# Computing a layernorm, linear-attention and feed-forward block with pairs of 64-row matmuls on TensorE

## The chip, the cores and the metric

The kernel runs on one core of one Trainium2 chip. The metric is the device time of one execution in microseconds (us). Lower is better. Repeated executions of one kernel on one chip mostly agree within 1 to 2%. Each call of experiments ran on its own chip, with the kernel before run between the others on the same chip. I therefore compare kernels of different calls by their ratio to the kernel before.

Engine names in the profile: PE is TensorE's matmul stream, PEld its weight loads, DVE VectorE, ACT ScalarE, POOL GpSimd. SP (SyncE) issues most DMAs.

## The reference, cut to what matters

```python
x  = A_x                                    # [1, 2048, 448] bf16
xn = layernorm(x)
# A: attention with a softmax feature map, 16 heads of 28
q, k, v = split(xn @ wqkv)                  # each 2048 x 448
pq, pk  = q @ w_phi[h], k @ w_phi[h]        # per head, 28 x 28
phi(p)  = concat(softmax(p), softmax(-p))   # 56 features a head
kv, z   = sum_s phi(pk) v,  sum_s phi(pk)
A = (phi(pq) @ kv / (phi(pq) @ z + 1e-6)) @ wo
# B: feed-forward
B = silu(xn @ w1) @ w2                      # 448 -> 1792 -> 448
out = x + A + B
```

The kernels fold `w_phi` into the q and k columns of `wqkv`, so pq and pk are direct products of xn. Six products over features remain: q, k, v, `wo` (all 448 to 448), ffn1 (448 to 1792) and ffn2 (1792 to 448).

## The kernel before

It records all operations, schedules them with a static list scheduler and emits each engine's stream. A matmul here uses up to 128 rows of TensorE's array (ffn2, `128*128` in the page). The 448 features are cut into 4 slices of 112 rows, so every product over 448 is four matmuls into one bank of PSUM, the memory that TensorE writes its results to. Some words used below: kv is the sum over tokens of phi(pk) times v, and of phi(pk) itself (z); KVZ is the step that readies both sums; U is phi(pq) times them; the fold is the product of `wqkv` and `w_phi`. A chunk is 512 tokens, and its exp phase is the work on q, k, v and kv, with ffn2 tiles in between. The late stage is U, `wo` and the last ffn2 tiles. Warm-up means matmuls whose results nobody uses. The parts that the argument touches:

```python
KT, KP = 4, 112
# ffn1: 4 matmuls of 256 or 512 tokens, one bank, one silu each
for kt in range(KT):
    e.matmul(hps, w1_sb[:, kt, ft*128:(ft+1)*128], xnT_sb[:, kt, tok0:tok0+ntok],
             start=(kt == 0), stop=(kt == KT - 1))
...
# k and v of a 128-token tile: 4 + 4 matmuls of 448 columns
e.matmul(pkb, xnT_sb[:, kt, t*128:(t+1)*128], Wfull[:, kt, D:2*D], ...)
e.matmul(vb,  xnT_sb[:, kt, t*128:(t+1)*128], Wfull[:, kt, 2*D:3*D], ...)
...
# q of 512 tokens, transposed by construction (weights stationary): 4 x 4 matmuls of 512
e.matmul(pqb, Wfull[:, kt, g*KP:(g+1)*KP], xnT_sb[:, kt, c*512:(c+1)*512], ...)
...
# kv and U: groups of four heads, 8 matmuls of 116 or 120 columns a tile (cross-head blocks masked)
# ffn2 of a tile: 14 matmuls of 128 rows x 448 columns; ACT evicts, POOL adds x
# wo of a tile: 4 matmuls of 448 columns into its own bank; DVE adds the ffn2 result
```

The softmax here doesn't subtract the row's maximum and nothing guards it: scores larger than these inputs give would overflow.

## Time and profile before

The median is 187.96 us (187.78 to 188.22, 5 runs). The profiled span is 185.7 us.

| | before |
|---|---|
| PE busy | 176.4 us, 95% of the span |
| ACT, DVE, POOL busy | 99.9, 96.0, 75.6 us |
| PE's share of the chain that ended last | 77% |
| a matmul of 448, 512 and 116 columns | 189, 215 and 53 ns |

From the page of the kernel before: the busy time of each engine, then the chain that ended last.

```profile
PE 176.4 (95%) x1272; PEld 105.1 (57%) x1272; DVE 96.0 (52%) x215; ACT 99.9 (54%) x197; POOL 75.6 (41%) x94
...
PE 77%; DVE 7%; DMA 6%; SPq 4%; POOL 2%; issue 1%; ACT 1%; POOLq 0%; DVEq 0%; ACTq 0%
```

A busy PE need not be at its full pace (below, pairs of 208 ns and of 109 ns both count as busy), so its pace has to be read from the timeline. Columns: start, length from the first start to the last modelled end, engine and line, operation, output and inputs, shapes, count.

```profile
70.65 0.92 PE L582 MATMUL psum<-Wfull,xnT_sb 112*128 112x448 bf16 x4
71.41 1.03 PE L627 MATMUL psum<-xnT_sb,Wfull 112*112 112x512 bf16 x4
72.27 0.92 PE L582 MATMUL psum<-Wfull,xnT_sb 112*128 112x448 bf16 x4
73.03 1.11 PE L640 MATMUL psum<-w_sb,hT 128*128 128x448 bf16 x5
73.98 0.92 PE L582 MATMUL psum<-Wfull,xnT_sb 112*128 112x448 bf16 x4
...
100.29 0.58 PE L604 MATMUL psum<-vaug,Ek 128*112 128x116 bf16 x8
100.71 0.54 PE L577 MATMUL psum<-Wfull,xnT_sb 112*128 112x448 bf16 x2
```

Take the distance between two starts and not the lengths, since the lengths overlap. Four matmuls of 448 columns take 71.41 - 70.65 = 0.76 us (chain view: the same), 189 ns each; four of 512 take 0.86 us, 215 ns each; eight of 116 take 0.42 us, 53 ns each. ffn2's five matmuls of 128 rows take 73.98 - 73.03 = 0.95 us, 190 ns each, like those of 112 rows. That is about 2.4 columns a nanosecond (2.2 for the short ones), and the number of rows in use does not enter. So the kernel pays for four slices of 112 rows what four slices of 128 would cost.

### The profile page before, as it was taken

To read this page: it belongs to the slowest core of one execution; us is meant where nothing else is said; L and a number is where in the kernel's file an instruction comes from. 1 tells how busy PE (TensorE), PEld (TensorE's weight loads), DVE (VectorE), ACT (ScalarE), POOL (GpSimd) and SP (SyncE) were. 2 spreads that over 40 slices of the span, in tenths; PEclk is the share of its full clock that TensorE was granted. 3 is DMA by queue.
4 is the path that set the end of the run, shared out by engine and by line. 5 is a ranking of instruction groups with operands and counts; after the bars stand their busy time and mean duration, and the time that the engine had idled before them with its cause. 6 is when DMAs were issued, how large, how long until landed. Compare 5 with 4: busy or idle time off the path is not lost.

```text
span 185.7 us, 3256 instructions
## 1 busy us (share of the span) xinstructions
PE 176.4 (95%) x1272; PEld 105.1 (57%) x1272; DVE 96.0 (52%) x215; ACT 99.9 (54%) x197; POOL 75.6 (41%) x94
## 2 busy tenths in 40 slices
PE   6978999999998999999999999999999999999982
PEld 6766866654444445556666666555555555555540
DVE  2439893050003000166777742478987888646762
ACT  2575496736663675838767765535444553513221
POOL 4136175000000000289888983165255235443651
PEclk9999999999999999999999999999999999999997
DMA  4999990000000000000000000001001000000011
GB/s 136 235 281 220 252 306 17 2 4 0 0 0 0 0 4 0 0 0 4 2 0 0 4 0 0 0 4 48 28 25 47 32 25 28 25 25 25 6 47 49
DMA packets 11375, 8.72 MB, mean 47 GB/s; under 512 B 992, under 2 KB 11360, under 8 KB 11360
## 3 DMA queue, kind: packets, MB, share of 16 engines
q1 hardware_dynamic: 11360, 8.51, 18.3%
q8 instruction: 10, 0.16, 0.4%
q14 instruction: 5, 0.04, 0.1%
HBM read 6.68 MB, written 1.84 MB: 46 GB/s over the span
## 4 chain that ended last, share of the span: by engine, by line
PE 77%; DVE 7%; DMA 6%; SPq 4%; POOL 2%; issue 1%; ACT 1%; POOLq 0%; DVEq 0%; ACTq 0%
PE psum L552 22%; PE psum L640 20%; PE psum L577 7%; PE psum L582 7%; DMA scr<-in_A_wqkv_dram 6%; PE psum L627 5%; PE psum L696 5%; SPq L445 4%; PE psum L604 4%; PE psum L660 3%; POOL scr L682 2%; DVE scr L676 2%; PE psum L688 2%; DVE den L669 1%; PE psum L513 1%
## 5 line engine op out<-in xcount | busy, mean ns | idle before, releaser
L552 PE MATMUL psum<-xnT_sb,w_sb 112*128 112x512 bf16 (+1 forms) x280 | 51.9, 337 | 0.8 <-ACT hT L555 0.5
L640 PE MATMUL psum<-w_sb,hT 128*128 128x448 bf16 x224 | 50.2, 352 | 0.8 <-DVE xnT_sb L541 0.6
L555 ACT ACTIVATE hT<-psum 128x256 bf16<-128x256 f32 (+1 forms) x70 | 34.4, 511 | 21.5 <-PE psum L552 21.0
L552 PEld LDWEIGHTS psum<-xnT_sb,w_sb 112*128 112x128 bf16 x280 | 26.4, 98 | 21.8 <-ACT hT L555 1.1
L645 POOL TENSOR_TENSOR Y_sb<-Y_sb,x_sb 128x448 f32<-128x448 f32 x16 | 16.5, 1033 | 52.9 <-ACT Y_sb L643 49.8
L592 DVE TENSOR_REDUCE Sk<-Ek 128x32 f32<-128x896 bf16 x16 | 17.3, 1084 | 28.4 <-ACT Ek L586 28.4
L682 POOL TENSOR_TENSOR scr<-scr 128x448 bf16<-128x448 f32 x16 | 18.1, 1134 | 33.7 <-DVE scr L676 25.3
L640 PEld LDWEIGHTS psum<-w_sb,hT 128*128 128x128 bf16 x224 | 21.0, 97 | 18.6 <-DVE xnT_sb L541 0.8
L596 POOL TENSOR_TENSOR Ek<-Ek,Rk 128x896 bf16<-128x896 bf16 x16 | 27.1, 1699 | 2.9 <-DVE Rk L594 1.7
L631 ACT ACTIVATE EqT<-psum 112x512 bf16<-112x512 f32 x32 | 17.6, 597 | 10.3 <-PE psum L627 10.3
L586 ACT ACTIVATE Ek<-psum 128x448 bf16<-128x448 f32 x32 | 15.6, 544 | 9.1 <-PE psum L577 5.0
L690 ACT ACTIVATE scr<-psum 112x512 bf16<-112x512 bf16 x16 | 9.5, 596 | 18.7 <-PE psum L688 18.7
L627 PE MATMUL psum<-xnT_sb,Wfull 112*112 112x512 bf16 x64 | 19.4, 379 | 0.0
L676 DVE TENSOR_TENSOR scr<-psum,Gq 128x896 f32<-128x896 f32 x16 | 17.4, 1090 | 0.7
L541 DVE COPY xnT_sb<-psum 112x512 bf16<-112x512 bf16 x12 | 4.8, 417 | 24.3 <-PE psum L535 24.3
L577 PE MATMUL psum<-Wfull,xnT_sb 112*128 112x448 bf16 x64 | 16.5, 352 | 0.0
L696 PE MATMUL psum<-wo_sb,scr 112*128 112x448 bf16 x64 | 14.8, 352 | 1.6 <-ACT scr L690 1.6
L643 ACT ACTIVATE Y_sb<-psum 128x448 f32<-128x448 f32 x16 | 8.8, 550 | 12.4 <-PE psum L640 5.8
L582 PE MATMUL psum<-Wfull,xnT_sb 112*128 112x448 bf16 x64 | 14.9, 352 | 0.0
L699 DVE TENSOR_TENSOR scr<-psum,Y_sb 128x448 bf16<-128x448 f32 x16 | 9.9, 620 | 6.9 <-POOL Y_sb L645 2.3
L521 DVE BATCH_NORM_STATS2 st<-x_sb 128x6 f32<-128x448 bf16 x16 | 9.6, 605 | 6.9 <-DMA x_sb<-in_A_x_dram 6.9
L665 DVE RECIPROCAL R<-psum 128x32 f32<-128x32 f32 x16 | 5.7, 357 | 11.7 <-PE psum L660 11.7
(48 smaller groups left out, 179.1 us busy)
## 6 DMA issues: line engine op xcount, KB each, us to landing
out_dram<-scr SPq DMA_DIRECT2D x16, 112.0 KB, 1.7
w_sb<-in_B_w_dram SPq DMA_DIRECT2D x7, 224.0 KB, 5.7
w_sb<-in_B_w_dram SPq DMA_DIRECT2D x1, 1568.0 KB, 14.9
x_sb<-in_A_x_dram SPq DMA_DIRECT2D x3, 448.0 KB, 8.1
scr<-in_A_wqkv_dram SPq DMA_DIRECT2D x1, 784.0 KB, 10.3
Wfull<-in_A_wqkv_dram SPq DMA_DIRECT2D x1, 392.0 KB, 10.3
wo_sb<-in_A_wo_dram SPq DMA_DIRECT2D x1, 392.0 KB, 11.0
x_sb<-in_A_x_dram SPq DMA_DIRECT2D x2, 112.0 KB, 2.4
```

The lines of the kernel that those rows point to most:

```text
L552: P.op("pe", d_mm(ntok), lambda e, lhsT=lhsT, rhs=rhs, hps=hps, kt=kt: e.matmul(hps, lhsT, rhs, start=(kt == 0), stop=(kt == KT - 1)), rea ...
L555: P.op("act", d_act(ntok), lambda e, dsth=dsth, hps=hps: e.activation(dsth, hps, ACTF.Silu), reads=[hps], writes=[dsth], table="silu", nam ...
L577: P.op("pe", d_mm(D), lambda e, lhsT=lhsT, rhs=rhs, pkb=pkb, kt=kt: e.matmul(pkb, lhsT, rhs, start=(kt == 0), stop=(kt == KT - 1)), reads= ...
L582: P.op("pe", d_mm(D), lambda e, lhsT=lhsT, rhs=rhs, vb=vb, kt=kt: e.matmul(vb, lhsT, rhs, start=(kt == 0), stop=(kt == KT - 1)), reads=[lh ...
L592: P.op("dve", d_dve(896), lambda e, E3=E3, sl=sl: e.tensor_reduce(Sk[:, sl, :], E3, AXL.X, ALU.add), reads=[E3], writes=[Sk[:, sl, :]], na ...
L596: P.op("pool", d_pool(896, 1.77), lambda e, E3=E3, sl=sl: e.tensor_tensor(E3, E3, Rk[:, sl, :, None].broadcast_to([128, 32, DH]), ALU.mult ...
L627: P.op("pe", d_mm(512), lambda e, lhsT=lhsT, rhs=rhs, pqb=pqb, kt=kt: e.matmul(pqb, lhsT, rhs, start=(kt == 0), stop=(kt == KT - 1)), read ...
L631: P.op("act", d_act(512), lambda e, dstE=dstE, pqb=pqb, s=s: e.activation(dstE, pqb, ACTF.Exp, scale=(1.0 if s == 0 else -1.0)), reads=[pq ...
L640: P.op("pe", d_mm(D), lambda e, lhsT=lhsT, rhs=rhs, ft=ft: e.matmul(fb, lhsT, rhs, start=(ft == 0), stop=(ft == FT - 1)), reads=[lhsT, rhs ...
L676: P.op("dve", d_dve(896), lambda e: e.tensor_tensor(dsto, U4[:, :, :, 0:DH], Gq[:, q, :].rearrange("p (s h) -> p s h", s=2)[:, :, :, None] ...
L682: P.op("pool", d_pool(448, 2.26), lambda e: e.tensor_tensor(o_sum[:, q, :], o_both[:, q, 0, :], o_both[:, q, 1, :], ALU.add), reads=[o_bot ...
L696: P.op("pe", d_mm(D), lambda e, lhsT=lhsT, rhs=rhs, g=g: e.matmul(ob, lhsT, rhs, start=(g == 0), stop=(g == G - 1)), reads=[lhsT, rhs], wr ...
```

## The change

The intent is to fill the array. The 448 features are cut into seven slices of 64 rows. The operands lie in both halves of the partitions, and two matmuls that use rows 0 to 63 and rows 64 to 127 and write two different banks are issued as a pair. If both run at once, one product over 448 costs 3.5 passes instead of 4. What else moves:

- q and k are one pair with tokens stationary. q then has to be transposed, which DMA does (16 times), as it does for xT of 12 of the 16 token tiles.
- Heads are handled in pairs of 56 features, so kv and U have 58 and 29 columns.
- POOL normalises q as well as k; this replaces the row sums that U carried before.
- ffn2's half sums of the late tiles stay in PSUM, and wo adds onto one of them.
- The scheduler keeps PE's order as written and places the other engines by latest start times.

The diff, cut to its core:

```diff
-        KT, KP = 4, 112
+    NS = D // 64
+        def pair(mms, n, name, dur=None):
+            def fn(e):
+                for (dst, lhsT, rhs, st, sp) in mms:
+                    ins = e.matmul(dst, lhsT, rhs, start=st, stop=sp, skip_group_check=True)
+                return ins
 ...
-            for kt in range(KT):                      # ffn1
-                lhsT = w1_sb[:, kt, ft * 128:(ft + 1) * 128]
+            for s in range(NS):
+                pair([(bank(2 * sl + q)[:, 0:n], w1_sb[HALF[q], s, i * 128:(i + 1) * 128],
+                       xT[HALF[q], c % NXC, s, j0 * 128:j0 * 128 + n], s == 0, s == NS - 1) for q in range(2)], n, "f1")
+            act(dst, src, ACTF.Silu, 2 * n, table="silu", name="silu")     # both banks at once
 ...
+            for s in range(NS):                       # q in the low half, k in the high half
+                pair([(bank(2 * sl + q)[:, 0:D], xT[HALF[q], c % NXC, s, j * 128:(j + 1) * 128], wqk[HALF[q], s, :],
+                       s == 0, s == NS - 1) for q in range(2)], D, "qk")
+            P.dma(lambda e: e.dma_start_transpose(out=phT[:, t], in_=E[:, e4, 0, :]), ...)
 ...
-                lhsT = hT[:, ft, t * 128:(t + 1) * 128]        # ffn2
+                pair([(bank(2 * sl + q)[:, 0:D], hT[HALF[q], c % NH, ft, j * 128:(j + 1) * 128], w2_sb[HALF[q], ft, :],
+                       ft == 0, ft == FT - 1) for q in range(2)], D, "f2")
 ...
+            if t >= 4:                                # xT
+                P.dma(lambda e: e.dma_start_transpose(out=dstx, in_=src), ...)
```

## The prediction

> **What bounds the kernel now: TensorE.** In the page's busy table PE is busy 176.4 of 185.7 us (95%); ACT, DVE and POOL 54%, 52%, 41%. PE is 77% of the chain that ended last, and the windows from 40 to 160 us show PE 97 to 100% busy at clock 1.00. So streamed columns are the price: in the chain, 4 matmuls of 448 columns take 0.76 us (189 ns each), of 512 columns 0.86 us (216 ns); 8 kv matmuls of 116 columns take 0.42 us in the timeline (53 ns each).
>
> **What the change removes.** A contraction over 448 is four passes of 112 rows. It becomes seven 64-row slices, two results at once on the two halves of the array: 3.5 passes per result. [...] no trace here shows it yet, and all rests on it. TensorE time, estimated from the slopes above, before to after in us:
> - ffn1 48.5 to 42.4
> - ffn2 42.4 to 42.4 (1792 rows fill the array anyway)
> - q and k 25.9 to 21.2; v 12.1 to 10.6; wo 12.1 to 10.6
> - kv and U 14 to about 7 (58 and 29 columns instead of 116 and 120)
> - transposes and fold about 13 to 4: xT for 12 of 16 tiles and all of q go through DMA
>
> Sum: 168 to 138, 30 us less, nearly all critical since PE has no slack.
>
> **What it adds.** POOL normalises q as well as k: 32 multiplies of 1.7 us (54 us, was 27). DVE sums 1792 columns a tile, about 2.0 us (1084 ns for 896 before). ACT keeps about 95 us, with about 7 table loads of 1.28 us, since exp and silu phases alternate. In an exp phase I estimate ACT 11.6 of 14.2 us of PE work, and over a chunk (25 us of PE) POOL about 20, DVE about 17: none bounds; slack is small where two exp phases meet (POOL about 33 of 28 us; six E buffers absorb it). The 28 DMA transposes hide behind other work. Summing ffn2 and wo in a bank only removes evictions.
>
> **Sum by stage (us from span start).** First real PE work near 6; first ffn1 chunk, fold and waits for w1 to about 22; first exp phase with a short wait for w2 (5.7 MB at about 255 GB/s lands near 24) to 37; three chunks of ffn1 and exp 75, plus 3 for phase switches, to 115; late stage 37 plus 1.5 for KVZ to 154; last addition and output to about 156. The measured time lies about 2 us above the span: 158 us.
>
> **The profile should show:** two matmuls of 448 columns per about 190 ns, overlapping; PE still the longest part of the chain; kv and U pairs near 27 ns; POOL 75 us or more; DVE near 100; clock about 1.00; idle PE mostly before 25 us (DMA) and at exp/silu switches (ACT).
>
> **What would make it wrong.** If pairs overlap only partly (say 1.7 times), matmul work grows by over 20 us and the gain vanishes. [...] If ACT evictions with three double slots hold PE, or POOL is slowed, exp phases stretch. DMA transposes queued behind big loads may come late. Perfect hiding: about 150.

## The result, and the profile after

The kernel after takes 158.19 us (median of 5 runs, 157.8 to 160.24, the longest slow) against 187.96. The ratio is 0.8436, 95% interval 0.8389 to 0.8484. All ratios here are computed as the mean time of one kernel's fast runs over that of the other's in the same rounds, so they are not quite the ratio of the medians quoted. The forecast was 158.0. On other chips the same kernel took 160.31 and 159.45 us, ratios 0.853 and 0.848. The profile below is of a run of 159.97 us, one of the longer ones; its span is 158.2 us, and the three fastest runs had spans of 156.1 to 156.5.

From the page of the kernel after: the busy times and the chain.

```profile
PE 147.7 (93%) x2242; PEld 93.9 (59%) x2242; DVE 94.0 (59%) x168; ACT 94.5 (60%) x120; POOL 83.9 (53%) x97
...
PE 90%; DMA 3%; DVE 3%; issue 1%; ACT 1%; DVEq 0%; SPq 0%
```

PE's busy time fell by 28.7 us, and the span by 27.5. PE now makes up 90% of the chain. The other engines carry about what they did; POOL rose by 8.3 us.

The timeline of the kernel after in its middle, same columns:

```profile
50.35 0.41 PE L426 MATMUL psum<-vb,E 64*128 64x58 bf16 x16
50.58 1.69 PE L426 MATMUL psum<-xT,w_sb 64*128 64x512 bf16 x14
52.09 0.41 PE L426 MATMUL psum<-vb,E 64*128 64x58 bf16 x16
52.32 1.69 PE L426 MATMUL psum<-xT,w_sb 64*128 64x512 bf16 x14
53.83 1.50 PE L426 MATMUL psum<-wqk,xT 64*128 64x448 bf16 x14
55.16 2.82 PE L426 MATMUL psum<-w_sb,hT 64*128 64x448 bf16 x28
57.80 0.54 PE L426 MATMUL psum<-wqk,xT 64*128 64x448 bf16 x3
```

Fourteen matmuls of 512 columns, seven pairs, take 53.83 - 52.32 = 1.51 us: 216 ns a pair. Seven pairs of 448 take 1.33 us (190 ns a pair), fourteen pairs of ffn2 2.64 us (189 ns a pair). A pair costs what one full-height matmul cost before. Eight kv pairs take 0.23 us, 29 ns each. The sixteen U pairs of a double tile take 0.41 us, 26 ns each (first and second row of the second fence under a2).

The windows of the kernel after, cut where PE's work changes. Columns: stretch, its length, busy time and instructions of each engine, PE clock, DMA share, GB/s.

```profile
0.00:29.11 29.11, 22.30 (x429) 19.37 (x430) 13.63 (x34) 15.18 (x26) 8.50 (x33) 0.94 0.95 253
29.11:42.34 13.23, 13.23 (x140) 7.97 (x142) 10.97 (x14) 10.16 (x14) 4.38 (x4) 1.00 0.60 84
42.34:117.68 75.34, 75.27 (x972) 43.13 (x969) 46.05 (x58) 57.09 (x65) 60.39 (x52) 1.00 0.45 79
117.68:154.62 36.94, 36.92 (x704) 23.44 (x704) 22.15 (x62) 12.09 (x18) 10.64 (x11) 1.00 0.14 47
154.62:158.20 3.58, 0.00 (x0) 0.00 (x0) 1.16 (x2) 0.00 (x0) 0.00 (x0) 0.90 0.34 128
```

Set against the stages of the prediction:

| stage | predicted us | measured us | difference |
|---|---|---|---|
| front: first ffn1 chunk, fold, loads | 22 | 29.1 | +7.1 |
| first exp phase | 15 | 13.2 | -1.8 |
| three chunks of ffn1 and exp | 78 | 75.3 | -2.7 |
| late stage with KVZ | 39 | 36.9 | -2.1 |
| end | 2 | 3.6 | +1.6 |

So the total hit because errors cancelled. From 29.1 us on PE waits for almost nothing (125.4 of 125.5 us busy), better than I had forecast. The front, however, is 7 us longer. Two questions follow. Is it really the concurrency of the two halves that pays? And what costs 7 us in the front?

The timeline of the front, with PE's idle time and its releaser in brackets:

```profile
1.63 3.59 PE L426 MATMUL psum<-ident 64*128 64x128 bf16 x64 [1.63 <-POOL neghalf L464]
7.12 0.56 PE L439 MATMUL psum<-ident,xnd 64*128 64x64 bf16 x14 [1.90 <-DVE xnd L545]
...
9.29 6.35 PE L426 MATMUL psum<-xT,w_sb 64*128 64x256 bf16 x70 [0.85 <-ACT xT L444]
15.47 0.38 PE L439 MATMUL psum<-ident,xnd 64*128 64x64 bf16 x14
15.67 0.94 PE L426 MATMUL psum<-xT,w_sb 64*128 64x256 bf16 x14
16.43 0.38 PE L439 MATMUL psum<-ident,xnd 64*128 64x64 bf16 x14
...
22.07 0.37 PE L426 MATMUL psum<-BD,phT 64*128 64x56 bf16 x15
24.39 0.22 PE L426 MATMUL psum<-BD,phT 56*128 56x56 bf16 x1 [1.96 <-issue]
```

Three things stand out. The 32 warm-up pairs of 128 columns take 3.59 us, 112 ns each, about half pace (a quarter of the 216 ns of a later pair of 512 columns is 54). The first 35 ffn1 pairs take 6.18 us to the next start at 15.47, where 35 x 109 = 3.8 us would be full pace (the group of 14 matmuls at 15.67 takes 0.76 us, 109 ns a pair). The windows show 26 matmuls from 9.3 to 12.0, 208 ns a pair. And at 22.3 us PE stops for about 2 us in the middle of a fold pair. "issue" means that the profile shows nothing that it waited for, and the built program has no semaphore wait at that matmul. The page's clock row drops to 0.5 in the slice that follows; the windows show 0.50 from 24.39 to 27.70 us.

### The profile page after: what moved, and what is told of

Its sections match the earlier page's. It is cut to its first block, busy times and chain, and to the rows that moved or that the text cites. A ratio compares the mean times of both kernels' runs of the same rounds, so it can differ in the third digit from the quotient of the medians.

```text
span 158.2 us, 5148 instructions
## 1 busy us (share of the span) xinstructions
PE 147.7 (93%) x2242; PEld 93.9 (59%) x2242; DVE 94.0 (59%) x168; ACT 94.5 (60%) x120; POOL 83.9 (53%) x97
## 4 chain that ended last, share of the span: by engine, by line
PE 90%; DMA 3%; DVE 3%; issue 1%; ACT 1%; DVEq 0%; SPq 0%
PE psum L426 88%; DMA x_sb<-in_A_x_dram 3%; PE psum L439 2%; DVE xnd L545 1%; DVE phT L747 1%; DVE st L532 0%; DVE x_sb L722 0%; ACT hT L444 0%; ACT xT L444 0%; DVEq L911 0%; SPq L454 0%; DVE mv L533 0%; DVE ve L535 0%
## 5 line engine op out<-in xcount | busy, mean ns | idle before, releaser
L608 POOL TENSOR_TENSOR E<-E,Rk 128x896 bf16<-128x896 bf16 x32 | 53.3, 1697 | 11.8 <-issue 5.2
L426 PE MATMUL psum<-xT,w_sb 64*128 64x512 bf16 (+1 forms) x490 | 50.6, 355 | 1.0 <-ACT xT L444 0.8
L426 PE MATMUL psum<-w_sb,hT 64*128 64x448 bf16 x448 | 45.2, 349 | 0.0
L444 ACT ACTIVATE hT<-psum 128x1024 bf16<-128x1024 f32 (+1 forms) x35 | 29.4, 853 | 13.1 <-PE psum L426 12.6
L426 PEld LDWEIGHTS psum<-xT,w_sb 64*128 64x128 bf16 x490 | 27.4, 101 | 15.9 <-issue 1.0
L426 PEld LDWEIGHTS psum<-w_sb,hT 64*128 64x128 bf16 x448 | 24.8, 94 | 16.4
L601 DVE TENSOR_REDUCE Sk<-E 128x64 f32<-128x1792 bf16 x16 | 31.9, 2011 | 2.6 <-ACT E L444 2.6
L444 ACT ACTIVATE E<-psum 128x896 bf16<-128x896 f32 x32 | 27.6, 914 | 7.5 <-PE psum L426 6.9
L444 ACT ACTIVATE xT<-psum 128x896 bf16<-128x896 bf16 (+2 forms) x20 | 13.0, 690 | 27.0 <-PE psum L439 24.7
L426 PE MATMUL psum<-wqk,xT 64*128 64x448 bf16 x224 | 24.0, 349 | 0.1
```

The source lines that it names most:

```text
L426: ins = e.matmul(dst, lhsT, rhs, start=st, stop=sp, skip_group_check=True)
L444: return P.op("act", d_act(n), lambda e: e.activation(dst, src, func, scale=scale), reads=reads or [src], writes=writes or [dst], table=ta ...
L601: dve(lambda e: e.tensor_reduce(Sk[:, t % 3, :].rearrange("p (h g) -> p h g", g=2), Er, AXL.X, ALU.add), d_dve(1792), [Er], [Sk[:, t % 3, ...
L608: pool(lambda e, Eh=Eh, Rb=Rb: e.tensor_tensor(Eh, Eh, Rb, ALU.mult), 1770, [Eh, Rh], [Eh], "phi%d" % qk)
```

## The experiments

Theory A and rival B are stated per run, before it ran.

### a1_one_half: both matmuls of a pair on the same rows

```diff
+        ROWS = (LO, LO)
-   ... xT[HALF[q], ...], wqk[HALF[q], s, :] ...      # likewise v, ffn2, wo
+   ... xT[ROWS[q], ...], wqk[ROWS[q], s, :] ...
```

> Both matmuls of each pair of the q/k, v, ffn2 and wo products read rows 0 to 63, so the two can no longer run side by side; instruction count, evictions and DMA stay the same (the result is wrong on purpose). ffn1, kv, U and the transposes keep their pairs. Theory A (the gain is that the two halves of the array run at once, fully): 448 pairs of 448 columns cost 2 x 189 ns instead of 189, so 448 x 0.189 = 85 us more, about 243 us. Rival B (the pair only costs as much because the matmuls are pipelined, in whatever rows; the gain over the kernel before comes from fewer evictions and the new order): about 158 us as in the kernel after.

It took 244.56 us (one run; relative error 0.023). Its output is wrong, which doesn't matter for the time. Timeline of a1:

```profile
29.07 2.81 PE L426 MATMUL psum<-wqk,xT 64*128 64x448 bf16 x14
31.72 5.46 PE L426 MATMUL psum<-w_sb,hT 64*128 64x448 bf16 x28
37.01 2.81 PE L426 MATMUL psum<-wqk,xT 64*128 64x448 bf16 x14
```

Seven pairs now take 2.65 us instead of 1.33, and fourteen 5.29 instead of 2.64: exactly double. With the same matmuls, evictions and transfers, the span grew by 84.6 us (242.8 against 158.2), and that came from one thing, that the two matmuls of a pair no longer used different rows. Rival B is out. The state of a single run is unknown, but fast and slow runs of one kernel differ by about 3% at most here, and this is 54%.

### a2_ffn2_full: ffn2 as one 128-row matmul per slice

```diff
-  pair([(bank(2*sl+q)[:, 0:D], hT[HALF[q], ...], w2_sb[HALF[q], ft, :], ...) for q in range(2)], D, "f2")
+  pair([(bank(2*sl+t%2)[:, 0:D], hT[:, ...], w2_sb[:, ft, :], ...)], D, "f2")
   # and no eviction, no DVE or POOL addition of the second half
```

> Only ffn2 goes back to one 128-row matmul per slice into one bank (right result), which also drops 8 ACT evictions, 8 DVE and 8 POOL additions. Theory A (a pair costs exactly one full-height matmul, so ffn2 gains nothing from being paired, and ACT, DVE and POOL have slack): within 1% of the kernel after, 157 to 159 us. Rival B [...]: 32 changes of mode, each perhaps 0.1 to 0.2 us [...] (its 349 ns record against the 189 ns step), so 3 to 6 us more, 161 to 165 us.

Rival B's 0.1 to 0.2 us a change was the author's estimate, from a matmul's record of 349 ns against its step of 189 ns.

163.97 us (162.05 to 164.76, 4 runs), ratio to before 0.866 [0.861, 0.872]; the kernel after had 0.844 to 0.853. Slower, as rival B said. Timeline of a2 in the late stage:

```profile
119.95 0.57 PE L426 MATMUL psum<-KVZ,phT 56*128 56x29 bf16 x32
120.46 2.82 PE L426 MATMUL psum<-w_sb,hT 128*128 128x448 bf16 x14
123.21 0.38 PE L439 MATMUL psum<-ident,xT 64*128 64x64 bf16 x14
```

The same place in the kernel after:

```profile
117.68 0.57 PE L426 MATMUL psum<-KVZ,phT 56*128 56x29 bf16 x32
118.09 2.82 PE L426 MATMUL psum<-w_sb,hT 64*128 64x448 bf16 x28
120.73 0.38 PE L439 MATMUL psum<-ident,xT 64*128 64x64 bf16 x14
```

From U to ffn2 it takes 0.51 instead of 0.41 us, and from ffn2 to the transposes 2.75 instead of 2.64: 0.10 to 0.11 us for each change of mode, which here means a step from 64-row to 128-row matmuls or back. What TensorE does in that time, no run shows. Over the windows from the first q/k tile to the last matmul a2 needs 128.8 us against 125.5, 3.3 us more; 32 changes at 0.10 us are 3.2. The other 0.6 us of the two spans' difference lies in the front, which is 29.7 us long in a2.

This is a reason to make *everything* on TensorE a pair. Pairing gains ffn2 nothing, since 14 pairs take what 14 full matmuls do (2.82 us in both timelines); it only avoids changes of mode.

### a3_x_on_pe: all xT tiles transposed on PE

```diff
-            if t >= 4:
+            if t >= 16:
```

> All 16 xT tiles are transposed on PE, none by DMA (right result). Theory A (PE is the limit, so each piece of PE work costs what it takes): 12 tiles x 7 pairs x 29 ns = 2.4 us more, plus up to 1 us of waits for double slots, 160 to 162 us. Rival B (the DMA transposes and their wide xnd copies cost the front something, so taking them away pays for the PE work): same or faster, 156 to 158 us.

168.2 us (168.02 to 168.67, 4 runs), ratio 0.895 [0.892, 0.898]. Both theories missed: this was 8 to 10 us slower. The transposes themselves cost what was forecast (14 matmuls in 0.20 us, 12 tiles, 2.4 us). The chain and the timeline of a3 show the rest as waits, because PE works strictly in the written order:

```profile
20.26 0.51 PE L439 MATMUL psum<-ident,xnd 64*128 64x64 bf16 x14 [2.55 <-DVE xnd L545]
...
45.99 0.38 PE L439 MATMUL psum<-ident,xnd 64*128 64x64 bf16 x14 [0.29 <-ACT E L444]
46.81 0.81 PE L439 MATMUL psum<-ident,xnd 64*128 64x64 bf16 x28 [0.43 <-ACT vb L444]
```

At 17.7 us PE stands for 2.55 us before a tile whose load has only just come. At the end of exp phases it queues for the PSUM slots that ACT still has to empty. By windows, the front is 3.0 us longer, the first exp phase 2.4, the chunks 2.4 and the late stage 0.4, 8.1 in all; 2.4 of that is PE work. The DMA transposes are thus worth more than the PE time they save: they take xT out of PE's order and out of the PSUM slots. I did not look for a better place for these transposes in PE's order, so this is an upper bound.

### a4_warm and b2_long_warm: more warm-up before ffn1

```diff
-        NWARM = 32                 # pairs of 128 columns
+        NWARM = 52                 # a4; and 4 and 12 more pairs behind the first two transposes
+        wide(13) ... X(0); wide(1); X(1); wide(2)      # b2: 16 pairs of 512 columns instead
```

> PE gets 52 warm-up pairs instead of 32, and 4 and 12 more after the first two tiles' transposes, so that it doesn't idle before ffn1 (right result). Theory A (the first ffn1 pairs took 208 ns instead of 109 because the PE clock was still half, after 1.9 us of idle PE from 5.2 us on): ffn1 starts at 109 ns a pair, about 2 us less in all, 156 us. Rival B (those pairs wait for w1 by DMA): no change, 158 us. Of the 2 us stop at 22.3 us in the middle of a fold pair: if it is bound to the place in PE's instruction stream (72 matmul instructions are added before it), it comes 72 matmuls earlier in the program, in ffn1; if it is bound to what that fold pair needs, it stays there; if it is chance, it may vanish.

> Warm-up by 16 pairs of 512 columns (13 at the start, 1 and 2 between the first transposes and ffn1) instead of 32 pairs of 128: longer warm-up with 32 matmuls fewer in PE's instruction stream. Theory A: ffn1's first pairs run at 109 ns instead of 208 (2 us less) and, with fewer instructions, PE reaches the missing ones later in the program, so the stop is not longer than now; 155 to 157 us. Rival B (the slow first pairs wait for w1, and what a4 lost was the price of longer warm-up): no gain, 158 to 160 us.

Both runs missed the times of both theories: 160.67 us for a4 (159.6 to 162.73, 6 runs, ratio 0.854) and 161.74 us for b2 (158.86 to 163.69, 6 runs, slow ones included; ratio of its only two fast runs 0.849 against 0.853 for the control b0, whose intervals overlap). The reason is in my edit. The schedule is made anew for each kernel, and it had changed DVE's order. Timeline of DVE in a4:

```profile
11.68 0.63 DVE L532 BATCH_NORM_STATS2 st<-x_sb 128x6 f32<-128x448 bf16 x1 [3.54 <-DMA x_sb<-in_A_x_dram]
12.22 0.37 DVE L571 COPY xT<-psum 128x448 bf16<-128x448 bf16 x1
```

The statistics of tile 2, waiting for their load until 11.68, had come to stand in front of the two copies (L571) that ffn1 needs. PE stood until 13.00, and its idle time was labelled "issue" although it was a wait for DVE. In the kernel after the copies run at 7.74 and 8.48. So these two runs say nothing about the clock; c2 below repeats the test. Nor do they say what the stop is bound to: in both profiles it is absent, but ffn1 began 3.7 and 2.7 us later there (at 13.00 and 11.98 us instead of 9.29). They do show that an "issue" label should be checked against the program's waits.

### b3_no_warm: no warm-up at all

```diff
-        NWARM = 32
+        NWARM = 0
```

> No warm-up at all, 64 matmuls fewer in front. Theory A: the clock is half at the start of ffn1 in the kernel after anyway, so nothing is lost there (at most 1 us, as the half clock may last longer), and PE reaches the missing instructions 64 matmuls later in the program, in the last fold groups or the first q/k tile, so the stop shrinks or vanishes; 156 to 159 us. Rival B (the warm-up works, the stop is bound to the fold): 2 us or more slower, 160 to 162 us, with the stop at the same fold pair.

159.57 us (158.84 to 161.49, 6 runs), ratio 0.848 against 0.853 for b0: no loss. The warm-up of the kernel after buys nothing: PE idles 1.9 us after it, and the next ffn1 pairs run at half pace in any case (208 ns instead of 109). Rival B is out. Of theory A only the first half held: the time is 0.6 us above its range, and the stop neither shrank nor came later in the program. It was 2.46 us long and came earlier, in the fold's transposes (counted below).

### b0_after_again, b1_w2_late, c0_control: the stop at 22 us

b0 and c0 are the kernel after, unchanged. b1 delays the 1.6 MB of w2 and the last x tiles:

```diff
-        load(w2_sb[:], ..., "w2", issue=1900)
-        load_x(8, 16)
...
+                # in the loop over ffn1 of tokens 256 to 511, before the fold:
+                P.dma(... w2 ..., reads=[hT[:, 0, 0, 256:512]], writes=[w2_sb[:]], ...)
+                load_x(8, 16)
```

> The kernel after, unchanged, as a control on this chip beside the next runs. Both theories: 157 to 160 us. Theory A (PE waits for its own instructions, which come by DMA behind the loads): the stop of about 2 us in the middle of the first fold group comes again at the same matmul, with a 16 KB fetch on the instruction queue started about 2.5 us before PE resumes. Rival B (a chance event of that one run): it doesn't come again, or elsewhere.

> The 1.6 MB of w2 and the last x tiles are loaded only after the first ffn1 piece of tokens 256 to 511 (about 20 us), so that the DMA engines have nothing to do for a moment just before the stop. Theory A: the instruction fetch isn't queued behind loads, starts earlier than 21.75 us, and the stop at the first fold group shrinks to under 0.5 us; ffn2 of tile 0 then waits for w2 instead, so the time is 158 to 162 us. Rival B (the stop has nothing to do with the loads): 2 us of stop in the same place.

> The kernel after, unchanged, beside the next two on the same chip: 158 to 161 us, with the stop in the first fold group, at a matmul that waits for no semaphore.

b0 took 160.31 us (158.61 to 162.82), c0 159.45 (159.07 to 162.21). In both the stop came again at the same matmul. Timeline of c0:

```profile
15.52 1.25 PE L426 MATMUL psum<-xT,w_sb 64*128 64x256 bf16 x15
17.03 1.69 PE L426 MATMUL psum<-xT,w_sb 64*128 64x256 bf16 x27 [0.26 <-issue]
...
22.02 0.37 PE L426 MATMUL psum<-BD,phT 64*128 64x56 bf16 x15
24.28 0.20 PE L426 MATMUL psum<-BD,phT 56*128 56x56 bf16 x1 [1.89 <-issue]
```

b1 took 157.14 us (156.32 to 157.33, 4 runs), ratio 0.835 [0.831, 0.839], against 0.853 [0.849, 0.857] for b0 on the same chip: 2% faster, and a little better than the 158 to 162 us of theory A. Timeline of b1:

```profile
22.07 0.37 PE L426 MATMUL psum<-BD,phT 64*128 64x56 bf16 x16
22.28 0.93 PE L426 MATMUL psum<-xT,w_sb 64*128 64x256 bf16 x14
...
25.48 1.50 PE L426 MATMUL psum<-wqk,xT 64*128 64x448 bf16 x14
27.63 2.82 PE L426 MATMUL psum<-w_sb,hT 64*128 64x448 bf16 x28 [0.66 <-DMA w_sb<-in_B_w_dram]
```

The stop is gone, and with it the half clock that followed. ffn2 waits 0.66 us for w2 instead. A rebuild of both programs shows the same order on PE throughout, and on DVE, ACT and POOL until after the stop. Half clock does not follow every stop: in b0 the clock was 1.00 from 24.66 us, after a stop of 1.88 us, where it was 0.64 in the kernel after and in c0.

Two more readings tie the stop to PE's own instructions. First, where it falls. Counting matmul records from the start, the two issue gaps of c0 come after the 219th and the 345th, and those of b3, which has 64 fewer in front, after the 218th (2.46 us) and the 343rd (0.41 us). In c0 the first gap is short (0.26 us) and the second long (1.89 us), in b3 the reverse. The place is bound to the position in the stream and not to the work. The distance of about 126 matmuls, each with its weight load, is about 252 instructions plus a few others. Second, the DMA view lists an instruction queue. This is its line in the quarter microsecond from 21.75 us in the kernel after (packets, MB, share of 16 engines' time):

```profile
q8 instruction: 1, 0.02, 27.6%
```

That packet takes 0.276 x 16 x 0.25 = 1.1 us of one engine and starts between 21.75 and 22 us; PE resumes about 2.5 us later. In b1 the same packet starts between 18.5 and 18.75 us, when the loads have thinned out (54 GB/s from 18.5 to 19 us, against 226 in the kernel after), and PE passes without a stop. The packets hold about 16 KB (0.28 MB in 17 on the page), and their number goes with PE's stream: the pages list 17 on q8 for the 4484 matmuls and weight loads of the kernel after and 10 for the 2544 of the kernel before, one for 264 and for 254 of them. That is close to the 252 between the two gaps, so I take q8 to bring PE's instructions, about 250 in a packet; this is an estimate from these counts. In the kernel after the stop fell among loads that ran at 253 GB/s over the front and at 414 from 21.75 to 24.25 us. That loads hold the fetch back is shown by b1. Whether the packet waits in a queue or is requested late, no run tells.

### c2_long_warm_kept, c1_combined, d1_reordered: both losses removed

c2 is b2 with DVE's order held (the copies before the statistics). c1 adds b1 and puts v before the first ffn2 tile. d1 also puts the statistics of tiles 4 to 7 behind the fold's copies.

```diff
+  bn_stats ..., ordered=od or t in (2, 3))                # c2; in d1: 2 <= t < 8
+  tensor_copy ..., name="xT_ev", ordered=t < 2)           # c2; in d1 also "fT_ev", ordered=True
+            if c == 0: V(t)                               # c1: before F2_early(f2[0])
-        for t in (4, 5): LN(t); X(t)                      # d1: moved behind the second ffn1 loop
```

> b2 again, with the order on DVE held as in the kernel after: in a4 and b2 the schedule, made anew, had put the statistics of tiles 2 and 3, which wait for a load, in front of the two evictions that ffn1 needs. Theory A (the half clock costs the first ffn1 pairs 2 us, and a4 and b2 lost by that order on DVE alone): ffn1 starts near 9 us at 109 ns a pair; up to 2 us less than the control, unless the stop for instructions grows by what PE gains, since the fetch is held back by the loads: then the gain is under 1 us, and the stop near 4 us. Rival B (longer warm-up itself does harm): slower than the control.

> c2 with w2 and the last x tiles loaded late (b1) and v of tiles 0 and 1 put before the first ffn2 tile. Theory A (half clock and held-back instructions are two separate losses of about 2 us each, with 1 to 2 us more of half clock after the stop): neither is left, 3 to 5 us less than the control, 154 to 156 us, unless ffn2 of tile 0 now waits for w2, at most 2 us. Rival B (the front is bound by the bytes that must land before the exp phase, whatever PE does): no better than b1, 157 us.

> c1 with the statistics of tiles 4 to 7, which wait for a load, put behind the fold's evictions on DVE; in c1 they stood in front, and PE waited 1.9 us for those evictions. Theory A (that order on DVE took back what the warm clock had gained): PE's wait of 1.9 us before the first fold group falls below 0.5 us, and q/k starts about 1.5 us earlier, near 24.5 us; part may come back as a wait for v or w2; 154.5 to 156.5 us, ratio to before 0.82 to 0.83. Rival B (from there on the loads of w2 set the pace): same as c1, ratio 0.833.

| kernel | median us (range, runs) | ratio to before [95%] |
|---|---|---|
| c0, the kernel after | 159.45 (159.07 to 162.21, 5) | 0.848 [0.845, 0.851] |
| c2 | 158.14 (157.34 to 158.5, 6) | 0.840 [0.838, 0.843] |
| c1 | 157.03 (155.83 to 158.75, 6) | 0.833 [0.829, 0.836] |
| d1, on another chip | 155.65 (154.81 to 157.59, 6) | 0.827 [0.823, 0.831] |

The times of c2 and d1 are as theory A had them. c1 missed its 154 to 156 us: its 0.833 is not clear of b1's 0.835, as its rival B had it. d1's interval overlaps c1's, and the record classes d1 as unclear; two of its six runs and four of the eleven of the kernel before in its call are marked slow, and the ratio is that of the others.

c2's ffn1 does run at full pace; timeline of c2:

```profile
8.65 3.23 PE L426 MATMUL psum<-xT,w_sb 64*128 64x256 bf16 x56 [0.29 <-ACT xT L444]
12.34 0.92 PE L426 MATMUL psum<-xT,w_sb 64*128 64x256 bf16 x13 [0.46 <-issue]
```

Twenty-eight pairs in 3.23 us, 115 ns each including the tail, where the kernel after needed 208 ns at first. So the slow start was the clock and not the loads of w1. The recorded clock says so too, though not in the profile of the kernel after (1.00 in its windows from 9.3 to 12.0 us, at 208 ns a pair): over the first 35 pairs it was 0.73 in b0 and in c0, over the first 28 of c2 1.00. What raises the clock, beyond the longer warm-up of c2, no run takes apart. But c2 gained only 1.3 us by the medians: PE reached its next waits earlier and stood there, 2.2 us before the fold, for DVE, and the clock was 0.71 from 21.25 us to the first q/k tile.

c1 stood there too, 1.9 us. DVE's in-order stream had the statistics of tiles 4 to 7, whose load came at 18.6 us, before the fold's copies, which ran from 20.9 us. d1 removes that order. The timeline of d1 at this place (its profile fell on a run marked slow, 157.19 us; only the order of events is read from it):

```profile
18.33 2.01 PE L426 MATMUL psum<-xT,w_sb 64*128 64x256 bf16 x27
20.20 0.38 PE L426 MATMUL psum<-BD,phT 64*128 64x56 bf16 x16
...
22.92 0.94 PE L426 MATMUL psum<-xT,w_sb 64*128 64x256 bf16 x14 [1.36 <-DVE wqk L774]
```

The wait before the fold is gone. 1.36 us came back at the next copy behind the same statistics, and 1.0 us later as a wait for an xT transpose. d1 has the lowest ratio, 2.4% below the kernel after (0.827 / 0.848; 2.0% against its first ratio, 0.844), and is correct. Of what is left in the front, the 1.36 us are again the order of work on an in-order engine.

## Why the prediction was right or wrong

1. **Two halves at once, 3.5 passes for 4: right.** Pairs of 448 and 512 columns take 189 and 216 ns, what one full matmul took before (189 and 215). a1 shows the cause: on the same rows a pair of 448 took 379 ns, twice as long. By the forecast's own sum the fuller array is 13.8 of the 30 us (ffn1 6.1, q and k 4.7, v and `wo` 1.5 each). The narrower kv and U make 7 (kv fell from 0.42 to 0.23 us a tile), and the transposes and the fold 9. No run takes these shares apart, except for 12 of the 28 DMA transposes (a3). That the two halves run at once was an assumption of the forecast; the pairs of the kernel after and a1 show it.
2. **Sum of PE's work, 168 to 138 us: right in the difference.** The forecast was 30 us less; PE's busy time fell 28.7, and the 147.7 us that remain still hold half-clock time of the front.
3. **Small pairs near 27 ns: right.** kv 29 ns, U 26 ns.
4. **ACT, DVE and POOL would not bound: right, and better than forecast.** From 29.1 to 154.6 us PE is busy 125.4 of 125.5 us. The 3 us for phase switches, the 1.5 us for KVZ and the wait for w2 (nearly 2 us of the forecast exp phase) did not occur; 6.6 us too much in three stages. POOL 83.9 us (75 or more forecast), DVE 94.0 (near 100), ACT 94.5 (95).
5. **"First ffn1 chunk, fold and waits for w1 to about 22": wrong, it was 29.1 us.** The step that failed is the front, and the cause I named, waiting for w1, was not it. In its place stand the half pace of the first ffn1 pairs (2.4 us: 35 pairs in 6.2 us instead of 3.8), the stop for instructions (2.0 us) with half clock after it (clock 0.64 over the 4.7 us that follow, about 1.7 us by that number), and PE's first real work at 7.1 us with 1.1 us of gaps to 9.3 where I had assumed 6. These make 8.3 us; the forecast front, 16 us from its first work for 10.6 us of ffn1 and the fold, had some room for waits. Their sizes vary from run to run: in b0 and c0 the first 35 pairs lost 1.4 us and not 2.4.
6. **The end: 3.6 us instead of 2.** I had counted the last addition and output too short.
7. **DMA transposes "hide behind other work": right, but I valued them only by PE's time.** Put on PE they cost 8 to 10 us and not 2.4 (a3).

Points 4 to 6 nearly cancel (-6.6, +7.1, +1.6), and the median run was about 2 us shorter than the profiled one, so the hit to 0.2 us is partly luck. The mechanism and the 30 us are not.

## What to carry to other kernels

A contraction that is not a multiple of 128 rows can be split into 64-row slices that run as pairs on the two halves of the array; a stream of such pairs costs per pair what one matmul costs (189 and 216 ns for 448 and 512 columns here), but each change between 64-row and 128-row matmuls cost 0.10 us here, so pair all or none of a stage. Once the middle of a kernel is free of waits, look at the front: a warm-up followed by idle time (1.9 us here) was lost (b3, without it, took 159.57 us against 160.31), a deep queue of early loads held back TensorE's own instructions (a stop of 2.0 us, gone in b1), and on an engine that works in the written order, as DVE did here, a statistic waiting for a load must not stand before a copy that TensorE needs (ffn1 began 3.7 us later in a4). After each edit to a statically scheduled kernel, compare the order of every engine before believing the time.
